# One decode step of attention beside a gated feed-forward: a scheduled kernel, and the same kernel programmed by hand with its own semaphores

## The chip, the cores and the metric

The kernel runs on one core of a Trainium2 chip. The metric is the device time of one execution in microseconds (us). The core has five engines that run their own instruction streams: PE (TensorE, matmuls), DVE (VectorE), ACT (ScalarE), POOL (GpSimd) and SP (SyncE, which here only issues transfers). Sixteen DMA engines move data from DRAM into the on-chip buffer SBUF, whose 128 partitions hold a row of each tile. PSUM is the small memory that matmuls write to.

## The reference, cut to what matters

```
x: (1, 1, 576)   k_cache, v_cache: (1, 32, 16384, 128)
wq: (576, 4096)  wo: (4096, 576)  w_gate, w_up: (576, 4608)  w_down: (4608, 576)     all float32

xn = layernorm(x)
q  = (xn @ wq) per head (32 heads of 128)
p  = softmax(q . k_cache * 128**-0.5)            # over 16384 positions, per head
o  = p @ v_cache
attention   = concat(o) @ wo
feedforward = (gelu(xn @ w_gate) * (xn @ w_up)) @ w_down
out = x + attention + feedforward
```

K and V are 8.39 MB each per head and are read once; with the weights (50.7 MB) that makes 587.6 MB.

## The kernel before

The kernel is written in a tile framework: pools give the buffers, and a scheduler puts in the semaphores. SBUF holds three big buffers of 64 KB a partition: `kslot` twice and `vslot` once. The pools put them at bytes 27904, 93440 and 158976 of a partition, each 256 bytes past a multiple of 512. All big loads are issued by SP, in the order of the program, through `load` (L78); a load whose buffer is still in use holds up those behind it.

First come the weights for q, gate and up. xn is spread over the partitions, PE computes q and the two halves of the feed-forward (`project`, L148), and ACT keeps q in `qrow`.

Then the loop over the 32 heads. K of head h goes into a K buffer, with 128 positions in each partition, in one load (the first head's in two halves of `SUB` = 64 positions). V of head h-1 is loaded into the V buffer right behind it; V of the last head goes into a K buffer instead. The steps of a head:

- `qk`: DVE multiplies K in place by q (L224), which `q_spread` (L163, PE) and `q_take` (L168, ACT) have spread over all partitions for four heads at a time, and sums over the 128 columns into the scores s (L225).
- `softmax`: DVE takes the maximum of s (L229), PE transposes it (L231), DVE takes the maximum over partitions, negated (L233), PE spreads that (L235), ACT scales it (L237) and computes the exponentials into pe (L238).
- `pv`: 32 matmuls on PE (L245) sum p times V into a PSUM bank po. Four heads share a bank: pe is laid out in steps of 16 columns, so that each head's results come to other partitions. There are two banks in turn.
- `out_heads`, after every fourth head: ACT copies the bank (L250), and four small matmuls pick the heads' outputs (L254), which ACT copies into `oall` (L255).

The tail loads w_down (36 rows of 576 a partition) and wo, and adds up rows times hT or oT on PE (L290). Two of the 32 rows of wo in each partition are loaded in another layout, the extra rows: fourteen small loads to 3, 6 or 8 partitions (`load_extra` L309, L320), which DVE sums up (L359, L362). The last rows of wo come in ever smaller loads. x is added at the end, and ACT issues the output.

Of the kernel before, what the change touches and what calls it, by code (L numbers as in the profile page):

```python
# [17 lines left out]
SUB = 64  # L18
# [4 lines left out]
HALF = D // 2  # L23
HD = H * DH
# [6 lines left out]
WD_PIECES = (16, 20)  # L31
WO_PIECES = (8, 8, 6, 4, 2, 1, 1)
WO_A = 8
WO_Q = 8
WO_M = 30
EX_K = 6
EX_H = 4 * EX_K
EX_REST = tuple((s, EX_H + 3 * i) for s in range(2) for i in range(2))
EX_LAST = H - 2
EX_N = 12  # L40
QUART = D // 4
HG = 4
PW = 4 * HG
PAD = 40
QH = 4
# [3 lines left out]
def kernel(ctx: ExitStack, tc: tile.TileContext, x, k_cache, v_cache, wq, wo, wg, wu, wd, out):  # L49
    nc = tc.nc  # L50
    cpool = ctx.enter_context(tc.tile_pool(name="cpool", bufs=1))
    kpool = ctx.enter_context(tc.tile_pool(name="kpool", bufs=2))
    vpool = ctx.enter_context(tc.tile_pool(name="vpool", bufs=1))
    spool = ctx.enter_context(tc.tile_pool(name="spool", bufs=2))
    ps_acc = ctx.enter_context(tc.tile_pool(name="ps_acc", bufs=1, space=bass.MemoryType.PSUM))
    ps_big = ctx.enter_context(tc.tile_pool(name="ps_big", bufs=1, space=bass.MemoryType.PSUM))
    ps_o = ctx.enter_context(tc.tile_pool(name="ps_o", bufs=1, space=bass.MemoryType.PSUM))
    ps_s = ctx.enter_context(tc.tile_pool(name="ps_s", bufs=2, space=bass.MemoryType.PSUM))
# [8 lines left out]
    wox = wo.rearrange("(h r t) f -> t h r f", r=4, t=WO_T)[WO_M:]  # L67
    wol = wo.rearrange("(p t) f -> t p f", t=WO_T)[WO_M:]
# [8 lines left out]
    def load(dst, src):  # L77
        nc.sync.dma_start(dst, src)  # L78
        return dst

    ROW3 = 3 * DF
    wq_t, wg_t, mix = kslot(), kslot(), vslot()
    load(wq_t, wmain["q"])
    qt = load(wg_t[:, ROW3 : ROW3 + QS], wtail["q"])
    row3, tails, at = {}, {}, 0
    for n in "gu":
        row3[n] = load(mix[:, at : at + DF], wmain[n][:, ROW3:])
        tails[n] = load(mix[:, at + DF : at + DF + DF // 2], wtail[n])
        at += DF + DF // 2

    xrow = mix[:1, ROW3 + FG : ROW3 + FG + D]
    nc.scalar.dma_start(xrow, xf)
    x2 = cpool.tile([P, HALF], F32, name="x2")
    nc.gpsimd.memset(x2, 0.0)
    for i in range(2):
        nc.scalar.dma_start(x2[32 * i : 32 * i + 1, :], xf[:, i * HALF : (i + 1) * HALF])

    ident = cpool.tile([P, P], F32, name="ident")
    make_identity(nc, ident)
    ones = cpool.tile([P, P], F32, name="ones")  # L100
    nc.vector.memset(ones, 1.0)
    eps_t = cpool.tile([P, 1], F32, name="eps_t")
    nc.vector.memset(eps_t, EPS)
    par = cpool.tile([P, 2], F32, name="par")
    nc.vector.tensor_reduce(par, ident.rearrange("p (d s) -> p s d", s=2), axis=AX.X, op=ALU.add)
    same = cpool.tile([P, 32], F32, name="same")
    nc.vector.tensor_reduce(same, ident.rearrange("p (q r) -> p r q", q=4), axis=AX.X, op=ALU.add)
    quarter = cpool.tile([P, 4], F32, name="quarter")
    nc.vector.tensor_reduce(quarter, ident.rearrange("p (q r) -> p q r", q=4), axis=AX.X, op=ALU.add)

    st = cpool.tile([1, 2, nc.vector.BN_STATS_DIM], F32, name="st")
    for i in range(2):
        nc.vector.bn_stats(st[:, i, :], xrow[:, i * HALF : (i + 1) * HALF])
    mv = cpool.tile([1, nc.vector.BN_AGGR_DIM], F32, name="mv")
    nc.vector.bn_aggr(mv, st)
    std = cpool.tile([1, 1], F32, name="std")
    nc.scalar.activation(std, mv[:, 1:2], AF.Sqrt, bias=eps_t[:1], scale=1.0)
    rstd = cpool.tile([1, 1], F32, name="rstd")
    nc.vector.reciprocal(rstd, std)
    nc.vector.tensor_scalar(xrow, xrow, mv[:, 0:1], rstd, op0=ALU.subtract, op1=ALU.mult)  # L120
    px = ps_s.tile([P, 512], F32, tag="sm", name="px")
    xm = xrow[:, :DM].rearrange("o (p j) -> o j p", j=DJ)
    for j in range(DJ):
        nc.tensor.matmul(px[:, j : j + 1], xm[:, j, :], ones[:1, :1], start=True, stop=True)
    xd = mix[:1, ROW3 + 2 * FG : ROW3 + 2 * FG + 2 * (D - DM)].rearrange("o (d s) -> o d s", s=2)
    nc.vector.tensor_copy(xd, xrow[:, DM:].unsqueeze(2).to_broadcast([1, D - DM, 2]))
    nc.tensor.matmul(px[:, DJ : DJ + 1], xd.rearrange("o d s -> o (d s)"), ones[:1, :1], start=True, stop=True)
    xp = cpool.tile([P, DJ + 1], F32, name="xp")
    nc.vector.tensor_copy(xp, px[:, : DJ + 1])
    xnb = cpool.tile([P, DJ, 32], F32, name="xnb")  # L130
    nc.vector.tensor_copy(xnb, xp[:, :DJ].unsqueeze(2).to_broadcast([P, DJ, 32]))
    xt = cpool.tile([P, 2], F32, name="xt")
    nc.vector.tensor_scalar(xt, par, xp[:, DJ:], None, op0=ALU.mult)
    xtb = cpool.tile([P, 2, 32], F32, name="xtb")
    nc.vector.tensor_copy(xtb, xt.unsqueeze(2).to_broadcast([P, 2, 32]))

    def project(steps, group, sizes):
        pg = ps_big.tile([P, 3, 512], F32, tag="pb", name="pg")
        for k, (j, rhs) in enumerate(steps):
            for b, size in enumerate(sizes):  # L140
                for q in range(4):
                    lo = q * group + sum(sizes[:b])
                    if j < DJ:
                        lhs = xnb[:, j, :]
                    else:
                        lhs = xtb[:, q // 2, :]
                        lo -= q // 2 * 2 * group
                    nc.tensor.matmul(pg[32 * q : 32 * q + 32, b, :size], lhs, rhs[:, lo : lo + size],  # L148
                                     start=k == 0, stop=k == len(steps) - 1)
        return pg  # L150

    steps = [(DJ, qt)] + [(j, wq_t[:, j * HD : (j + 1) * HD]) for j in range(DJ)]
    pq = project(steps, QG, (QB, QB))[:, :2, :]
    qrow = cpool.tile([P, QG], F32, name="qrow")
    nc.scalar.activation(qrow.rearrange("p (b f) -> p b f", f=QB), pq, AF.Copy)

    Q = {}

    def q_spread(h):
        r = 32 * (h // (H // 4))  # L160
        lo = h % (H // 4) * DH
        pq = ps_s.tile([P, 512], F32, tag="sm", name="pq")
        nc.tensor.matmul(pq, ones[r : r + 1, :], qrow[r : r + 1, lo : lo + QH * DH], start=True, stop=True)  # L163
        return pq

    def q_take(h, pq):
        qs = spool.tile([P, QH, DH], F32, name="qs", bufs=1)
        nc.scalar.activation(qs.rearrange("p h d -> p (h d)"), pq, AF.Copy)  # L168
        for i in range(QH):
            Q[h + i] = qs[:, i : i + 1, :]  # L170
# [87 lines left out]
    for h in range(H + 1):  # L258
# [12 lines left out]
        if h == 0:  # L271
            ffn_act()
# [139 lines left out]
```

## Time and profile before

| | |
|---|---|
| time, median of 3 runs | 1366.81 us (1366.80 to 1368.43) |
| span of the profiled execution (no other time is listed for it) | 1366.7 us |
| DVE busy | 1146.5 us, 84% |
| PE busy | 402.5 us, 29% |
| ACT busy | 36.8 us, 3% |
| load queue q1 | 587.60 MB, 99.4% of 16 engines' span |
| mean rate of reading | 430 GB/s |

The page lists busy times, DMA queues and groups of instructions; the timeline lists single instructions with their start and duration, and in brackets how long the engine had been idle before and what released it. A row of "SPq" or "ACTq" is the issue of a transfer, and the transfer's landing shows as the start of the instruction that waited for it. "x64" for 32 matmuls is right: a float32 matmul is two passes.

### The profile page before, as it was taken

To read this page: it belongs to the slowest core of one execution; us is meant where nothing else is said; L and a number is where in the kernel's file an instruction comes from. 1 tells how busy PE (TensorE), PEld (TensorE's weight loads), DVE (VectorE), ACT (ScalarE), POOL (GpSimd) and SP (SyncE) were. 2 spreads that over 40 slices of the span, in tenths; PEclk is the share of its full clock that TensorE was granted. 3 is DMA by queue.
4 is the path that set the end of the run, shared out by engine and by line. 5 is a ranking of instruction groups with operands and counts; after the bars stand their busy time and mean duration, and the time that the engine had idled before them with its cause. 6 is when DMAs were issued, how large, how long until landed. Compare 5 with 4: busy or idle time off the path is not lost.

```text
span 1366.7 us, 6440 instructions
## 1 busy us (share of the span) xinstructions
PE 402.5 (29%) x2876; PEld 119.1 (9%) x2876; DVE 1146.5 (84%) x189; ACT 36.8 (3%) x129; POOL 1.6 (0%) x8
## 2 busy tenths in 40 slices
PE   3331132332322232332212332322212232322164
PEld 1110000100000000100000000100000000000021
DVE  1069999989888888899888888898888888998843
ACT  0000000000000000000000000000000000000000
POOL 0000000000000000000000000000000000000000
PEclk9775655655655566555555566566556656566578
DMA  9999999999999999999999999999999999999997
GB/s 406 439 441 437 428 430 430 436 430 442 435 428 432 441 432 432 436 435 432 430 440 430 436 432 442 432 430 433 428 437 436 443 430 430 428 435 436 443 421 316
DMA packets 12180, 588.00 MB, mean 430 GB/s; under 512 B 1395, under 2 KB 1401, under 8 KB 2042
## 3 DMA queue, kind: packets, MB, share of 16 engines
q1 hardware_dynamic: 12140, 587.60, 99.4%
q8 instruction: 22, 0.36, 0.1%
q14 instruction: 4, 0.03, 0.0%
q10 hardware_dynamic: 14, 0.01, 0.0%
HBM read 587.60 MB, written 0.00 MB: 430 GB/s over the span
## 4 chain that ended last, share of the span: by engine, by line
DMA 52%; DVE 46%; PE 1%; issue 0%; SPq 0%; DVEq 0%; ACT 0%
DMA kslot<-in_A_k_cache_dram 41%; DVE s L225 23%; DVE kslot L224 23%; DMA kslot<-in_A_v_cache_dram 3%; DMA kslot<-in_B_w_up_dram 3%; DMA kslot<-in_B_w_down_dram 2%; DMA kslot<-in_A_wq_dram 2%; DMA kslot<-in_A_wo_dram 1%; PE pg L148 1%; SPq L78 0%; PE pt L231 0%; DVE vslot L185 0%; SPq L309 0%; DVE pm L229 0%; DVE nm L233 0%
## 5 line engine op out<-in xcount | busy, mean ns | idle before, releaser
L224 DVE TENSOR_TENSOR kslot<-kslot,qs 128x16384 f32<-128x16384 f32 (+1 forms) x33 | 551.3, 16705 | 83.6 <-DMA kslot<-in_A_k_cache_dram 83.6
L225 DVE TENSOR_REDUCE s<-kslot 128x128 f32<-128x16384 f32 (+1 forms) x33 | 551.2, 16703 | 3.7 <-DVE kslot L224 0.5
L245 PE MATMUL po<-vslot,pe 128*16 128x512 f32 x1984 | 285.5, 740 | 632.6 <-DMA vslot<-in_A_v_cache_dram 632.6
L245 PEld LDWEIGHTS po<-vslot,pe 128*16 128x16 f32 x1984 | 67.3, 113 | 835.3 <-issue 835.3
L231 PE MATMUL pt<-ident,pm 128*1 128x128 f32 x32 | 11.9, 372 | 244.5 <-DVE pm L229 244.5
L185 DVE TENSOR_TENSOR vslot<-pg,same 128x396 f32<-128x396 f32 (+1 forms) x6 | 3.0, 551 | 70.2 <-PE pg L148 70.2
L148 PE MATMUL pg<-kslot,xnb 128*32 128x396 f32 (+2 forms) x208 | 22.0, 583 | 21.1 <-DMA kslot<-in_B_w_gate_dram 17.8
L237 ACT ACTIVATE nb<-pb 128x1 f32<-128x1 f32 x32 | 5.5, 171 | 808.4 <-PE pb L235 808.4
L231 PEld LDWEIGHTS pt<-ident,pm 128*1 128x1 f32 x32 | 2.5, 79 | 267.9 <-DVE pm L229 227.0
L235 PE MATMUL pb<-nm,ones 1*128 1x1 f32 x64 | 18.1, 350 | 13.2 <-DVE nm L233 13.2
L233 DVE TENSOR_REDUCE nm<-pt 1x1 f32<-1x128 f32 x32 | 8.9, 279 | 15.0 <-PE pt L231 15.0
L235 PEld LDWEIGHTS pb<-nm,ones 1*128 1x128 f32 x64 | 15.8, 305 | 22.2 <-DVE nm L233 11.3
L163 PE MATMUL pq<-qrow,ones 1*128 1x512 f32 x16 | 15.6, 1073 | 0.0
L359 DVE TENSOR_SCALAR qrow<-qrow,ex 32x576 f32<-32x576 f32 x1 | 0.5, 507 | 15.4 <-DMA qrow<-in_A_wo_dram 15.4
L238 ACT ACTIVATE pe<-s,nb 128x128 f32<-128x128 f32 x32 | 12.8, 402 | 1.0
L329 DVE RECIPROCAL rl<-pl 128x32 f32<-128x32 f32 x1 | 0.4, 358 | 13.7 <-PE pl L327 13.7
L250 ACT ACTIVATE o<-po 128x512 f32<-128x512 f32 x8 | 4.8, 597 | 220.8 <-PE po L245 220.8
L148 PEld LDWEIGHTS pg<-kslot,xnb 128*32 128x32 f32 x208 | 7.1, 124 | 36.5 <-DMA kslot<-in_B_w_gate_dram 18.6
L254 PE MATMUL pc<-same,o 128*128 128x4 f32 x64 | 8.4, 255 | 5.7 <-ACT o L250 5.7
L229 DVE TENSOR_REDUCE pm<-s 128x1 f32<-128x128 f32 x32 | 9.2, 286 | 1.1
L362 DVE SCALAR_TENSOR_TENSOR qrow<-vslot,ex,qrow 24x576 f32<-24x576 f32 (+1 forms) x12 | 9.7, 806 | 0.4
L290 PE MATMUL acc<-kslot,oT 128*1 128x144 f32 (+1 forms) x108 | 8.5, 334 | 3.1 <-DMA kslot<-in_A_wo_dram 3.1
(89 smaller groups left out, 123.1 us busy)
## 6 DMA issues: line engine op xcount, KB each, us to landing
kslot<-in_A_k_cache_dram SPq DMA_DIRECT2D x2, 4096.0 KB
kslot<-in_B_w_gate_dram SPq DMA_DIRECT2D x1, 6912.0 KB
kslot<-in_B_w_up_dram SPq DMA_DIRECT2D x1, 6912.0 KB
kslot<-in_B_w_down_dram SPq DMA_DIRECT2D x1, 5760.0 KB
vslot<-in_B_w_down_dram SPq DMA_DIRECT2D x1, 4608.0 KB
kslot<-in_A_wo_dram SPq DMA_DIRECT2D x2, 2304.0 KB
vslot<-in_B_w_gate_dram SPq DMA_DIRECT2D x1, 2304.0 KB
vslot<-in_B_w_up_dram SPq DMA_DIRECT2D x1, 2304.0 KB
```

Of the source, the lines that this page charges most:

```text
L148: nc.tensor.matmul(pg[32 * q : 32 * q + 32, b, :size], lhs, rhs[:, lo : lo + size], start=k == 0, stop=k == len(steps) - 1)
L163: nc.tensor.matmul(pq, ones[r : r + 1, :], qrow[r : r + 1, lo : lo + QH * DH], start=True, stop=True)
L224: tc.keep_in_program_order(nc.vector.tensor_mul(blk, blk, Q[h].to_broadcast([P, n, DH])))
L225: nc.vector.tensor_reduce(S[h][:, i : i + n], blk, axis=AX.X, op=ALU.add)
L229: tc.keep_in_program_order(nc.vector.reduce_max(pm, S[h], axis=AX.X))
L231: nc.tensor.transpose(pt[:1, :P], pm, ident)
L233: tc.keep_in_program_order(nc.vector.tensor_reduce(nm, pt[:1, :P], axis=AX.X, op=ALU.max, negate=True))
L235: nc.tensor.matmul(pb[:, :1], ones[:1, :], nm, start=True, stop=True)
L238: nc.scalar.activation(pe4, S.pop(h).rearrange("p (k s) -> p k s", s=4), AF.Exp, bias=nb, scale=SCALE, accum_out=lsum[:, h : h + 1])
L245: nc.tensor.matmul(PO[h // HG % 2][q : q + PW, :], pe[:, lo : lo + PW], vt[:, k * 512 : (k + 1) * 512], start=i == 0 and k < 4, stop=i == ...
L290: tc.keep_in_program_order(nc.tensor.matmul(g, lhs, w[:, i * n : (i + 1) * n], start=id(g) not in seen, stop=last))
L362: nc.vector.scalar_tensor_tensor(ex_sum[:n], ex_rows[j][:n], ex[:n, j : j + 1], ex_sum[:n], op0=ALU.mult, op1=ALU.add)
```

## The change

The framework's scheduler is left aside. Every buffer has a fixed address, the three big ones (`A`, `B`, `C`) at 28672, 94208 and 159744, multiples of 4096 bytes. Each engine's program is written out by itself, with semaphores of its own: `take` waits for a semaphore and counts it down, `give` counts it up, and `done` makes an engine wait for its own last instruction. SP, ACT, PE and DVE loop over the heads (`Fori`; SP and DVE two heads to a trip), with the head's number in a register. K goes to B (even heads) and A (odd heads), V to C, the last V too. The first K is one load. q is spread a head at a time: ACT picks one head's q from all of them (`q_pick`), PE spreads it (`q_spread`), ACT copies it to qs. pe has no gaps and PO is one bank; each head's output is copied and picked by itself. There are no extra rows of wo: all 32 rows go through PE, w_down into B and A, wo into A and C.

SP's list of transfers at the end of the loop over the heads and in the tail. Before, where K30, V29, K31, V30 and V31 come first:

```order
L78 DMA kslot<-in_A_k_cache_dram 128x16384 [waits DMAHW5_49,DVE_49]
L78 DMA vslot<-in_A_v_cache_dram 128x16384 [waits DMAHW0_49,PE_49]
L78 DMA kslot<-in_A_v_cache_dram 128x16384 [waits DMAHW7_49,DVE_49]
L309 DMA vslot<-in_A_wo_dram 6x4x576 [waits DMAHW2_49,PE_49]
L309 DMA vslot<-in_A_wo_dram 6x4x576 x3
L78 DMA vslot<-in_B_w_down_dram 128x9216
```

(The first of these rows is K31, the third V31, and the small loads of wo and the first part of w_down follow.) After, from the end of SP's loop, where fa, fb and fv say that slot A, B or C is free:

```order
L129 DMA slot_a<-in_A_k_cache_dram 128x16384
L129 DMA slot_c<-in_A_v_cache_dram 128x16384 [waits fv_13]
L213 REGISTER_ALU
L213 COMPARE_AND_BRANCH
L129 DMA slot_c<-in_A_v_cache_dram 128x16384 [waits fv_13]
L129 DMA slot_b<-in_B_w_down_dram 128x16128 [waits fb_12]
L129 DMA slot_a<-in_B_w_down_dram 128x4608 [waits fa_11]
L129 DMA slot_a<-in_A_wo_dram 128x11520
L129 DMA slot_c<-in_A_wo_dram 128x3456 [waits fv_13]
```

V31 (the first row behind the loop) waits for the buffer that V30 is in, no longer for a K buffer, and w_down stands behind it.

DVE's work for a head in the body, before:

```order
L224 TENSOR_TENSOR kslot<-kslot,qs 128x16384 [waits DMAHW7_49]
L225 TENSOR_REDUCE s<-kslot 128x128 [waits DVE_49,Activation_49]
L229 TENSOR_REDUCE pm<-s 128x1 [waits DVE_49]
L233 TENSOR_REDUCE nm<-pt 1x1 [waits PE_49]
L224 TENSOR_TENSOR kslot<-kslot,qs 128x16384 [waits DMAHW1_49]
```

After, one trip of its loop (kb and ka: K has landed, qr: q is spread, sf: given by PE's first V matmul of the head before):

```order
L188 TENSOR_TENSOR slot_b<-slot_b,qs 128x16384 [waits kb_9,qr_33]
L191 TENSOR_REDUCE s<-slot_b 128x128 [waits own_63,sf_39]
L193 TENSOR_REDUCE pm<-s 128x1 [waits own_63]
L195 TENSOR_REDUCE nm<-bank 1x1 [waits pt_35]
L188 TENSOR_TENSOR slot_a<-slot_a,qs 128x16384 [waits ka_8,qr_33]
L191 TENSOR_REDUCE s<-slot_a 128x128 [waits own_63,sf_39]
L193 TENSOR_REDUCE pm<-s 128x1 [waits own_63]
L195 TENSOR_REDUCE nm<-bank 1x1 [waits pt_35]
L331 REGISTER_ALU
L331 COMPARE_AND_BRANCH
```

The reduce waited for ACT's exponentials of the head before, and now waits for PE, whose first V matmul comes behind them and behind V's landing.

The diff, cut to its core:

```diff
-    def kslot():
-        return kpool.tile([P, R * DH], F32, tag="k", name="kslot")
-    def vslot():
-        return vpool.tile([P, R * DH], F32, tag="v", name="vslot")
...
+SLOTS = (28672, 94208, 159744)
+WD_A, WO_A = 28, 20
+WO_C = (6, 3, 2, 1)
+WO_Q = 6
...
+def take(eng, s, n=1):
+    eng.wait_ge(s, n).then_inc(s, -n)
+def give(eng, s, n=1):
+    eng.sem_inc(s, n)
+def done(eng, inst):
+    ...
+    inst.then_inc(s, 1)
+    take(eng, s)
...
+def q_pick(h):
+    ACT.activation(qh, qd4.rearrange("p j t -> p (j t)"), AF.Copy, scale=whose[:, bass.ds(h, 1)]).then_inc(s_r, 1)
+def q_spread():
+    take(PE, s_r)
+    PE.matmul(pqb[:, :DH], ones, qh, start=True, stop=True).then_inc(qp, 1)
+def dve_head(k, slot, s_k, s_f):
+    kt = slot.rearrange("p (n d) -> p n d", d=DH)
+    take(DVE, s_k, 16)
+    take(DVE, qr)
+    done(DVE, DVE.tensor_mul(kt, kt, qs.unsqueeze(1).to_broadcast([P, R, DH])))
+    give(DVE, qd)
+    take(DVE, sf)
+    done(DVE, DVE.tensor_reduce(S, kt, axis=AX.X, op=ALU.add))
+    give(DVE, s_f)
+    DVE.reduce_max(pm, S, axis=AX.X).then_inc(s_pm, 1)
+    take(DVE, s_pt)
+    DVE.tensor_reduce(nm, ptb[:1, :P], axis=AX.X, op=ALU.max, negate=True).then_inc(s_nm, 1)
...
+        take(SP, fB)
+        load(B, kv[0], kB)
+        take(SP, fA)
+        load(A, kv[1], kA)
+        take(SP, fV)
+        load(C, vv[0], vL)
+        with SP.Fori(0, H // 2 - 1) as i:
+            take(SP, fB)
+            load(B, kv[bass.ds(2 * i + 2, 1)].rearrange("a p f -> (a p) f"), kB)
+            take(SP, fV)
+            load(C, vv[bass.ds(2 * i + 1, 1)].rearrange("a p f -> (a p) f"), vL)
+            take(SP, fA)
+            load(A, kv[bass.ds(2 * i + 3, 1)].rearrange("a p f -> (a p) f"), kA)
+            take(SP, fV)
+            load(C, vv[bass.ds(2 * i + 2, 1)].rearrange("a p f -> (a p) f"), vL)
+        take(SP, fV)
+        load(C, vv[H - 1], vL)
+        take(SP, fB)
+        load(B[:, : WD_A * D], wdv[:, : WD_A * D], s_tail[0])
+        take(SP, fA)
+        load(A[:, : (WD_T - WD_A) * D], wdv[:, WD_A * D :], s_tail[1])
+        load(A[:, wo_a : wo_a + WO_A * D], wov[:, : WO_A * D], s_tail[2])
+        take(SP, fV)
+        lo = WO_A
+        for k, n in enumerate(WO_C):
+            load(C[:, (lo - WO_A) * D : (lo - WO_A + n) * D], wov[:, lo * D : (lo + n) * D], s_tail[3 + k])
+            lo += n
...
+        with ACT.Fori(0, H) as h:
+            q_pick(h + 1)
+            take(ACT, qp)
+            take(ACT, qd)
+            ACT.activation(qs, pqb[:, :DH], AF.Copy).then_inc(qr, 1)
+            take(ACT, s_pb)
+            done(ACT, ACT.activation(nb, ptb[:, 256:257], AF.Copy, scale=SCALE))
+            ACT.activation(pe, S, AF.Exp, bias=nb, scale=SCALE, accum_out=lsum[:, bass.ds(h, 1)]).then_inc(s_ex, 1)
+            take(ACT, s_pv)
+            ACT.activation(o4, PO, AF.Copy).then_inc(s_o4, 1)
+            take(ACT, s_pc)
+            done(ACT, ACT.activation(oall[:, bass.ds(h, 1)], pcb[:, :1], AF.Copy))
...
+        with DVE.Fori(0, H // 2):
+            dve_head(0, B, kB, fB)
+            dve_head(1, A, kA, fA)
...
+        with PE.Fori(0, H):
+            q_spread()
+            take(PE, s_pm)
+            PE.transpose(ptb[:1, :P], pm, ident).then_inc(s_pt, 1)
+            take(PE, s_nm)
+            PE.matmul(ptb[:, 256:257], ones[:1, :], nm, start=True, stop=True).then_inc(s_pb, 1)
+            take(PE, s_ex)
+            take(PE, vL, 16)
+            for k in range(32):
+                q = 32 * (k % 4)
+                i = PE.matmul(PO[q : q + 4, :], pe[:, 4 * k : 4 * k + 4], C[:, k * 512 : (k + 1) * 512],
+                              start=k < 4, stop=k >= 28)
+                if k == 0:
+                    i.then_inc(sf, 1)
+            i.then_inc(s_pv, 1)
+            take(PE, s_o4)
+            for j in range(4):
+                i = PE.matmul(pcb[:, :1], o4[:, j * DH : (j + 1) * DH], same[:, j : j + 1], start=j == 0, stop=j == 3)
+                if j == 0:
+                    i.then_inc(fV, 1)
+            i.then_inc(s_pc, 1)
```

More of the change, by code (lines that the diff above doesn't have):

```diff
@@ L58, with small @@
-    ps_s = ctx.enter_context(tc.tile_pool(name="ps_s", bufs=2, space=bass.MemoryType.PSUM))
+    PE, DVE, ACT, SP, PL = nc.tensor, nc.vector, nc.scalar, nc.sync, nc.gpsimd
+    at = {"low": LOW, "high": HIGH}
+    def small(name, shape, where="low"):
+        n = 4
+        for s in shape[1:]:
+            n *= s
+        h = nc.alloc_sbuf_tensor_at(name, list(shape), F32, offset=at[where])
+        at[where] += (n + 31) // 32 * 32
+        assert at["low"] <= SLOTS[0] and at["high"] <= 229344
+        return h.ap()
@@ new lines, in slot @@
+    def slot(name, i):
+        return nc.alloc_sbuf_tensor_at(name, [P, SLOT], F32, offset=SLOTS[i]).ap()
+    A, B, C = slot("slot_a", 0), slot("slot_b", 1), slot("slot_c", 2)
+    bank = [nc.alloc_psum_tensor(f"bank{i}", [P, 512], F32).ap() for i in range(8)]
+    ident = small("ident", [P, P])
+    ones = small("ones", [P, P])
+    x2 = small("x2", [P, HALF])
+    eps_t = small("eps_t", [P, 1])
+    par = small("par", [P, 2])
+    same = small("same", [P, 32])
+    quarter = small("quarter", [P, 4])
@@ L157 @@
[L157 to L170, printed above, removed]
```

515 lines of the change are left out of this document (237 added, 278 removed).

## Prediction

> **What bounds the kernel now.** First the parts of the page on engines and DMA queues.
>
> ```profile
> span 1366.7 us, 6440 instructions
> ...
> PE 402.5 (29%) x2876; PEld 119.1 (9%) x2876; DVE 1146.5 (84%) x189; ACT 36.8 (3%) x129; POOL 1.6 (0%) x8
> ...
> q1 hardware_dynamic: 12140, 587.60, 99.4%
> q8 instruction: 22, 0.36, 0.1%
> ```
>
> Queue q1, where SP puts all its loads, keeps the 16 DMA engines busy for 99.4% of the span (1358 us); DVE, the busiest compute engine, has 16% left. The table of windows says how fast the stream is in the body (first row) and in the last two stages; the last two numbers of a row are DMA share and GB/s.
>
> ```profile
> 307.30:1237.50 930.20, 258.59 (x1668) 71.62 (x1668) 840.23 (x97) 24.18 (x90) 0.00 (x0) 0.61 1.00 434
> ...
> 1295.50:1314.80 19.30, 10.63 (x67) 2.83 (x67) 15.72 (x3) 0.67 (x3) 0.00 (x0) 0.68 0.98 423
> 1314.80:1363.10 48.30, 31.54 (x386) 12.42 (x386) 12.53 (x25) 1.24 (x6) 0.00 (x0) 0.83 0.91 383
> ```
>
> In the body the queue never rests: share 1.00 at 434 GB/s. The last window has 0.91: there some engines rest. Then the list of waits, and the row of the V matmuls:
>
> ```profile
> DVE kslot L224 <- DMA kslot<-in_A_k_cache_dram: 83.6, 27, 4.4
> PE po L245 <- DMA vslot<-in_A_v_cache_dram: 632.6, 31, 23.1
> ...
> L245 PE MATMUL po<-vslot,pe 128*16 128x512 f32 x1984 | 285.5, 740 | 632.6 <-DMA vslot<-in_A_v_cache_dram 632.6
> ```
>
> DVE and PE wait for K and V, not the reverse. So the time is bytes over rate plus every moment in which the queue has nothing to do, and the change has to be judged by one question: when does it let the queue run dry? One head from the timeline shows the margins.
>
> ```profile
> 496.44 0.33 SPq L78 DMA_DIRECT2D kslot<-in_A_k_cache_dram  x1
> ...
> 500.55 17.23 DVE L224 TENSOR_TENSOR kslot<-kslot,qs 128x16384 f32<-128x16384 f32 x1 [3.08 <-DMA kslot<-in_A_k_cache_dram]
> 517.88 17.22 DVE L225 TENSOR_REDUCE s<-kslot 128x128 f32<-128x16384 f32 x1
> ...
> 519.96 8.34 PE L245 MATMUL po<-vslot,pe 128*16 128x512 f32 x64 [20.35 <-DMA vslot<-in_A_v_cache_dram]
> ...
> 528.36 0.33 SPq L78 DMA_DIRECT2D vslot<-in_A_v_cache_dram  x1
> 535.13 0.33 SPq L78 DMA_DIRECT2D kslot<-in_A_k_cache_dram  x1
> 535.14 0.29 DVE L229 TENSOR_REDUCE pm<-s 128x1 f32<-128x128 f32 x1
> ...
> 535.89 0.28 DVE L233 TENSOR_REDUCE nm<-pt 1x1 f32<-1x128 f32 x1 [0.47 <-PE pt L231]
> ...
> 539.21 17.22 DVE L224 TENSOR_TENSOR kslot<-kslot,qs 128x16384 f32<-128x16384 f32 x1 [3.05 <-DMA kslot<-in_A_k_cache_dram]
> ...
> 558.55 9.52 PE L245 MATMUL po<-vslot,pe 128*16 128x512 f32 x64 [21.69 <-DMA vslot<-in_A_v_cache_dram]
> ```
>
> A K lands at 500.55, a V at 519.96, the next K at 539.21, the next V at 558.55: 19.3 us each, 38.6 a head (16.78 MB at 434 GB/s). The V issued at 528.36 comes 10.8 us before the transfer ahead of it is done (539.21); the K issued at 535.13 comes 23.4 before 558.55.
>
> **The body after the change.** Two waits move.
>
> The V buffer now comes free only after ACT has copied PO and PE has done the first of four picking matmuls, every head. The tail of before shows both at L250 and L254 (rows below): 0.72 us from the last V matmul to the picks, and a quarter of 1.05 us. So V is issued 1.0 us later, with 9.8 of 10.8 left: nothing, as long as K's transfer covers it; past that each us would cost 31, one for every V.
>
> The reduce of head h now waits for the first V matmul of head h-1 (semaphore sf). Behind it on DVE stand the maximum, the negation and the next product; SP's next K waits for it too. At 740 ns a pass, two passes overlapping, I take 1.0 us: the reduce starts at 521.0 instead of 517.88, ends at 538.2, and maximum, transpose and negation (535.14 to 536.17 in before) end at 539.3. The next K is there at 539.21, so the next product starts 0.1 to 0.5 late, ends by 557, and the reduce behind it waits for V anyway (558.55 + 1.0). The lag does not grow. K is issued near 538.3, 20 us early. DVE's own work for a head is 34.45 + 1.03 + gaps, about 35.8; the engine's waits on itself (the gap at 517.78 to 517.88 is 0.1) may make that 36.2. That leaves 2.4 us a head, 4.9 per trip of DVE's loop, which takes two heads.
>
> Spreading q each head puts a pick and a copy on ACT and a small matmul on PE behind the V matmuls. Bounded by the rows of the 512-wide spread and copy of before
>
> ```profile
> L163 PE MATMUL pq<-qrow,ones 1*128 1x512 f32 x16 | 15.6, 1073 | 0.0
> ...
> 518.22 0.60 ACT L168 ACTIVATE qs<-pq 128x512 f32<-128x512 f32 x1 [19.37 <-DVE kslot L224]
> ```
>
> this is at most 0.6 + 1.1 + 0.6 after 528.3 + 0.7 + 1.05 + 0.2, so qs is ready by 532.6, 6.6 us before the product at 539.21. Nothing either, and below nothing is excluded, since the queue is already full.
>
> **The start.** K0 is one load, not two halves, so DVE starts on the whole.
>
> ```profile
> 0.74 0.85 SPq L78 DMA_DIRECT2D kslot<-in_A_wq_dram  x2
> ...
> 75.55 7.63 PE L148 MATMUL pg<-kslot,xnb 128*32 128x396 f32 x72 [3.38 <-DMA kslot<-in_B_w_up_dram]
> ...
> 121.80 0.33 SPq L78 DMA_DIRECT2D kslot<-in_A_k_cache_dram  x1
> ...
> 133.56 8.69 PE L245 MATMUL po<-vslot,pe 128*16 128x512 f32 x64 [8.79 <-DMA vslot<-in_A_v_cache_dram]
> ```
>
> The up weights land at 75.55, K0 19.3 later at 94.9; product and reduce end near 129.7, and K2 is issued there instead of at 121.80. V0 lands at 133.56, 3.9 us later. An issue into an empty queue needs a lead. The chain of waits prices it:
>
> ```profile
> 1.18 23.69 DMA kslot<-in_A_wq_dram
> 24.86 0.14 issue
> ```
>
> Issued from 0.74, the 9.44 MB of wq are there at 24.86: 24.1 us, where 434 GB/s would need 21.7, so 2.4 us of lead. 3.9 covers it: cost 0, at most 1. From there DVE is a buffer behind and gains 2.4 a head; K3 (issued near 165.6, V1 due at 172.2) is already safe. The entry of the hand-written part has one more meeting of the engines: 0 to 0.7 us. Fewer instructions to fetch: all 0.36 MB of q8 are 0.8 us of the stream, so 0 to -0.8. I take nought for these together.
>
> **The tail** is where the change bites.
>
> ```profile
> 1272.06 0.33 SPq L78 DMA_DIRECT2D kslot<-in_A_v_cache_dram  x1
> ...
> 1295.51 9.68 PE L245 MATMUL po<-vslot,pe 128*16 128x512 f32 x64 [21.78 <-DMA vslot<-in_A_v_cache_dram]
> ...
> 1305.25 3.27 SPq L309 DMA_DIRECT2D vslot<-in_A_wo_dram  x4
> ...
> 1314.84 8.55 PE L245 MATMUL po<-kslot,pe 128*16 128x512 f32 x64 [2.49 <-DMA kslot<-in_A_v_cache_dram]
> ...
> 1323.46 0.60 ACT L250 ACTIVATE o<-po 128x512 f32<-128x512 f32 x1 [10.37 <-PE po L245]
> 1324.11 1.05 PE L254 MATMUL pc<-same,o 128*128 128x4 f32 x8 [0.72 <-ACT o L250]
> ...
> 1357.25 0.41 PE L290 MATMUL acc<-kslot,oT 128*1 128x288 f32 x2 [1.36 <-DMA kslot<-in_A_wo_dram]
> ...
> 1357.49 0.41 PE L290 MATMUL acc<-kslot,oT 128*1 128x288 f32 x2
> ...
> 1363.13 0.43 PE L290 MATMUL acc<-kslot,oT 128*1 128x144 f32 x8 [0.28 <-DMA kslot<-in_A_wo_dram]
> ```
>
> Before, the last V (V31) goes into a K buffer: issued at 1272.06, it follows V30 without a gap (1295.51, 1314.84). After, it goes into slot C, where V30 is being used, and SP's queue is in order: the weights of the tail, whose slot B has long been free, stand behind V31's wait. Between V30's landing and V31's issue nothing is queued. V31 is issued after PE's matmuls of head 30 and the copy and pick: 1295.51 + 9.68 + 1.0 = 1306.2. It starts an empty queue, so it lands 2.4 + 19.3 later, at 1327.9 instead of 1314.84: **+13.1**. Ends: the matmuls took 8.34 to 9.68 in the rows shown, and the lead may be down to 1.0, since part of the 2.4 may belong to the very first transfer. That gives 10.4 to 13.1, and I take the upper, whose rows are nearest.
>
> What follows V31 are wd and wo, 20.05 MB. Before takes 1314.84 to 1363.13, 48.3 us, in the window of share 0.91, among them fourteen loads into 3 to 8 partitions each. After has loads of 128 partitions only, all but the last four queued behind V31 before it lands, those four when V31 is used up, some 38 us ahead of their turn: 46.2 us at 434 GB/s, **-2.1**. Ends: nought, and -4.3 if the whole idle 9% of the window comes back. PE does not become late: two rows of weights take 0.24 us (1357.25 to 1357.49), so the 20 rows of wo that now land together need 2.4, at half pace 4.8, while the 12 rows behind them stream for 8.2. From the last landing to the end it is as before, 1366.7 - 1363.13 = 3.6.
>
> **Sum:** 1366.7 + 13.1 - 2.1 = **1377.7** (1327.9 + 46.2 + 3.6). The span is 0.1 below the median of the runs, so the same holds for the time.
>
> **Rivals.** *The aligned buffers pay for the gap.* Before has all three slots 256 bytes past a multiple of 512; after has them at multiples of 4096. If this alone made the stream 1% faster, 1358 us would shrink by 13.6 and the time would be 1364.1, faster than before. It decides from 0.8% (11.0 of 1358). For it: no transfer of before is aligned, so no row excludes it. Against it: the body stands at one steady rate with share 1.00. [...] Chance 0.02 for faster, 0.04 for a gain that lands within 0.2%.
>
> *The loops become the bound.* If each trip of DVE's loop (two heads) had to fetch its instructions again, one block of q8 costs 0.1% of 16 x 1366.7 over 22 blocks, 1.0 us, and 2.4 of lead, 3.4 in all: under the 4.9 that DVE has to spare. Two blocks in turn are 6.8, 1.9 too long, times 16 trips: 30 us, about 1408. [...] Chance 0.08.
>
> *The gap is covered all the same*, because the tail regains the 4.3, the lead is 1.0 and the matmuls 8.3: 1366.7 + 10.4 - 4.3 = 1372.8, still slower; only with a gain in the stream beside it would this be no change. Chance 0.02 for that.
>
> **The numbers.** Forecast 0.84, slow loops 0.08, the rest 0.08. About 0.2% (2.7 us) is what a measurement can tell from no change: faster 0.03, same 0.05, slower 0.92. The range takes in the low ends of the tail (1372.8) and, above, a tail that regains nothing with the start's 1.0 and 0.7 (1381.5), widened by the spread of a run or so: 1372 to 1383. The loops lie outside.
>
> **What would show it.** Right: in the windows a body at share 1.00 and 434, then a hole of about 12 us between the landing of V30 and the first bytes of V31, with SP waiting for PE; DVE's reduce waiting on PE for 3 us a head. Wrong: share below 0.99 in the body (loops, or a buffer freed late), a rate above 437 (alignment), or V31 landing 19.3 us after V30.

## The result, and the profile after

The hand-written kernel is slower by 1.2%.

| | before | after |
|---|---|---|
| time, median | 1367.62 us (1366.80 to 1368.44, 4 runs) | 1383.91 us (1382.73 to 1384.42, 4 runs) |
| ratio, with 95% interval | | 1.0116 (1.0101 to 1.0130) |
| span of the profiled execution | 1366.7 us | 1381.9 us (time 1383.64) |

First the page of after: engines, the moved gigabytes in 40 slices, and the queues.

```profile
span 1381.9 us, 8013 instructions
...
PE 442.0 (32%) x3104; PEld 171.5 (12%) x3104; DVE 1141.0 (83%) x173; ACT 71.5 (5%) x231; POOL 1.0 (0%) x7
...
GB/s 401 435 442 419 435 429 438 425 438 431 436 434 433 438 431 434 438 427 438 434 433 438 431 436 433 433 440 429 436 438 427 438 431 436 436 431 438 258 413 320
...
q1 hardware_dynamic: 11376, 587.60, 98.4%
q8 instruction: 5, 0.08, 0.0%
```

DVE stays as it was (83% of the span); PE and ACT do a little more and have most of the span free (32% and 5% busy). The queue does not stay: 99.4% of the span has become 98.4%, and one slice near the end stands at 258 GB/s. The table of windows is cut at that place. The moments of the first and last bytes, here and below, are from the trace's single DMA records, which no view prints; the last three numbers of a row are granted PE clock, DMA share and GB/s.

```profile
307.30:1237.50 930.20, 283.60 (x1849) 111.45 (x1849) 844.84 (x98) 50.73 (x168) 0.00 (x0) 0.61 1.00 434
...
1293.90:1306.60 12.70, 11.00 (x72) 4.25 (x72) 10.24 (x1) 0.77 (x2) 0.00 (x0) 0.76 0.00 0
...
1358.30:1367.00 8.70, 0.02 (x3) 0.05 (x7) 0.00 (x0) 0.00 (x0) 0.00 (x0) 0.68 0.91 392
1367.00:1374.20 7.20, 7.20 (x84) 2.38 (x88) 0.00 (x0) 0.00 (x0) 0.00 (x0) 0.67 0.86 356
```

From 307 us on, the body has the share and the rate of before (1.00, 434). Then comes a window of 12.7 us without a byte. In the last two rows PE is idle for 8.7 us and then busy for all of 7.2, at 0.67 of its clock. The timeline of after names both places. ("<-PEq L118" only says that the engine's own program waited in `take`, which is L118; for which semaphore stands in the program. "x48" merges rows of two forms: six rows in halves, four matmuls each, and three in quarters, eight each.)

```profile
1294.34 9.98 PE L377 MATMUL bank<-slot_c,pe 128*4 128x512 f32 x64 [17.18 <-PEq L118]
...
1304.45 0.60 ACT L266 ACTIVATE o<-bank 128x512 f32<-128x512 f32 x1 [26.30 <-ACTq L118]
1305.19 1.02 PE L384 MATMUL bank<-same,o 128*128 128x1 f32 x8 [0.87 <-PEq L118]
1305.65 0.34 SPq L129 DMA_DIRECT2D slot_c<-in_A_v_cache_dram  x1
1306.10 0.36 SPq L129 DMA_DIRECT2D slot_b<-in_B_w_down_dram  x1
...
1327.63 8.60 PE L377 MATMUL bank<-slot_c,pe 128*4 128x512 f32 x64 [11.87 <-PEq L118]
...
1366.98 7.37 PE L401 MATMUL bank<-slot_a,oT 128*1 128x288 f32 x80 [8.69 <-PEq L118]
1374.17 2.36 PE L401 MATMUL bank<-slot_c,oT 128*1 128x288 f32 x48
...
1377.54 0.92 PE L401 MATMUL bank<-slot_c,oT 128*1 128x144 f32 x24
1378.63 0.31 DVE L347 COPY ot<-bank 128x144 f32<-128x144 f32 x1 [1.59 <-DVEq L118]
```

V30 lands at 1294.34; V31 is issued at 1305.65, when PE is through with V30 and the first pick (L384) has given the slot back; w_down (slot_b), whose buffer was free all along, follows at 1306.10. V31 lands at 1327.63. At the end the 20 rows of wo keep PE from 1366.98 to 1374.17, so that at 1374.87, when the last byte comes, it has only begun the nine rows before the last three.

### The profile page after: what moved, and what is told of

Read it like the earlier page. It is cut to its first block, busy times and chain, and to the rows that moved or that the text cites. A ratio compares the mean times of both kernels' runs of the same rounds, so it can differ in the third digit from the quotient of the medians.

```text
span 1381.9 us, 8013 instructions
## 1 busy us (share of the span) xinstructions
PE 442.0 (32%) x3104; PEld 171.5 (12%) x3104; DVE 1141.0 (83%) x173; ACT 71.5 (5%) x231; POOL 1.0 (0%) x7
## 3 DMA queue, kind: packets, MB, share of 16 engines
q1 hardware_dynamic: 11376, 587.60, 98.4%
## 5 line engine op out<-in xcount | busy, mean ns | idle before, releaser
L377 PE MATMUL bank<-slot_c,pe 128*4 128x512 f32 x2048 | 296.4, 738 | 491.6 <-PEq L118 491.6
L191 DVE TENSOR_REDUCE s<-slot_a 128x128 f32<-128x16384 f32 x16 | 275.5, 17220 | 35.5 <-DVEq L118 35.5
L191 DVE TENSOR_REDUCE s<-slot_b 128x128 f32<-128x16384 f32 x16 | 275.5, 17220 | 31.5 <-DVEq L118 31.5
L188 DVE TENSOR_TENSOR slot_b<-slot_b,qs 128x16384 f32<-128x16384 f32 x16 | 275.6, 17225 | 8.4 <-DVEq L118 8.4
L188 DVE TENSOR_TENSOR slot_a<-slot_a,qs 128x16384 f32<-128x16384 f32 x16 | 275.6, 17226 | 0.0
L377 PEld LDWEIGHTS bank<-slot_c,pe 128*4 128x4 f32 x2048 | 84.7, 99 | 676.2 <-issue 664.5
L266 ACT ACTIVATE o<-bank 128x512 f32<-128x512 f32 x32 | 19.1, 597 | 761.1 <-ACTq L118 761.1
L384 PE MATMUL bank<-same,o 128*128 128x1 f32 x256 | 32.7, 249 | 28.3 <-PEq L118 28.3
L384 PEld LDWEIGHTS bank<-same,o 128*128 128x128 f32 x256 | 31.0, 191 | 57.1 <-issue 57.1
L182 PE MATMUL bank<-qh,ones 128*128 128x128 f32 x66 | 20.4, 402 | 54.6 <-PEq L118 54.6
```

Of the source, the lines that this page charges most:

```text
L182: PE.matmul(pqb[:, :DH], ones, qh, start=True, stop=True).then_inc(qp, 1)
L188: done(DVE, DVE.tensor_mul(kt, kt, qs.unsqueeze(1).to_broadcast([P, R, DH])))
L191: done(DVE, DVE.tensor_reduce(S, kt, axis=AX.X, op=ALU.add))
L266: ACT.activation(o4, PO, AF.Copy).then_inc(s_o4, 1)
L377: i = PE.matmul(PO[q : q + 4, :], pe[:, 4 * k : 4 * k + 4], C[:, k * 512 : (k + 1) * 512], start=k < 4, stop=k >= 28)
L384: i = PE.matmul(pcb[:, :1], o4[:, j * DH : (j + 1) * DH], same[:, j : j + 1], start=j == 0, stop=j == 3)
```

## The experiments

All in one table; the span is the median of a kernel's runs, "last byte" and "end behind it" are of its profile. The first four runs of after have a median span of 1382.15, the second four, which the differences below start from, 1380.9: a difference of 1 us between two sets of four is not clear of the noise. Before was run beside each: its spans have a median of 1366.4 us (19 runs in the first set), in two groups near 1365 and 1366.4.

| kernel | time | ratio to before (95%) | span | last byte | end behind it |
|---|---|---|---|---|---|
| before | 1368.15 | | 1366.4 | 1362.75 | 4.0 |
| after, run again | 1382.77 | 1.0107 (1.009 to 1.0123) | 1380.9 | 1374.71 | 6.9 |
| V31 in slot B | 1369.21 | 1.0011 (1.0001 to 1.002) | 1367.45 | 1360.12 | 7.4 |
| w_down ahead of V31 | 1369.84 | 1.002 (1.001 to 1.0031) | 1367.7 | 1360.25 | 6.0 |
| wo in pieces | 1381.46 | 1.0101 (1.0084 to 1.0118) | 1379.7 | 1374.19 | 5.4 |
| V31 in B, wo in pieces | 1366.81 | 0.9993 (0.9984 to 1.0002) | 1365.0 | 1359.79 | 5.5 |
| the same, filled (4 groups) | 1366.68 | 0.9990 (0.9981 to 0.9999) | 1364.9 | 1360.76 | 4.7 |
| the same, filled (1 group) | 1382.72 | 1.0109 (1.0093 to 1.0124) | 1380.95 | 1359.67 | 20.5 |
| before, V31 in its V buffer | 1371.64 | 1.0033 (1.0021 to 1.0045) | 1369.85 | 1365.95 | 4.0 |
| the same, order forced | 1382.0 | 1.0102 (1.0086 to 1.0118) | 1380.2 | 1375.80 | 4.1 |
| loops written out | 1386.79 | 1.0138 (1.0122 to 1.0153) | 1384.9 | 1377.62 | 6.8 |
| slots unaligned | 1382.7 | 1.0114 (1.0097 to 1.0131) | 1380.95 | 1374.26 | 6.9 |
| reduce released by ACT | 1382.72 | 1.0106 (1.009 to 1.0122) | 1380.65 | 1373.69 | 6.8 |

**V31 into slot B.** w_down's first part goes to C instead, and the last rows of wo to B.

```diff
-        take(SP, fV)
-        load(C, vv[H - 1], vL)
         take(SP, fB)
-        load(B[:, : WD_A * D], wdv[:, : WD_A * D], s_tail[0])
+        load(B, vv[H - 1], vZ)
+        take(SP, fV)
+        load(C[:, : WD_A * D], wdv[:, : WD_A * D], s_tail[0])
...
-        with PE.Fori(0, H):
+        with PE.Fori(0, H - 1):
+            pe_head(C, vL)
+        pe_head(B, vZ)
```

> The last V goes into slot B, free since head 30's reduce, and w_down's first part into C. My theory (the hole in the queue behind V30 costs 13 to 14 us, and PE is late in the tail besides): V31 lands 19.3 us after V30, near 1313.7 instead of 1327.6, and everything behind it comes as much earlier: span near 1368.0. Rival (the cost lies in the body, its loops, semaphores or per-head work): V31's place changes little, span near 1381.

The windows of this run, from V30's landing to V31's, and to the last byte:

```profile
1294.40:1313.70 19.30, 11.22 (x74) 4.16 (x74) 16.80 (x1) 1.45 (x4) 0.00 (x0) 0.68 1.00 434
1313.70:1360.10 46.40, 29.76 (x311) 10.20 (x315) 3.29 (x9) 1.63 (x6) 0.00 (x0) 0.75 0.96 411
```

V31 comes 19.3 us behind V30 at share 1.00, and the last byte comes 14.75 us earlier than in after. The span is 1367.5 in the profile: the rival with its 1381 falls. But the last byte is now 2.6 us earlier than in before, and the span is 1.0 longer: the end behind the last byte, 7.4 against 4.0, is a second cost.

**w_down ahead of V31.** V31 stays in slot C; only the order of two issues is changed.

```diff
-        take(SP, fV)
-        load(C, vv[H - 1], vL)
         take(SP, fB)
         load(B[:, : WD_A * D], wdv[:, : WD_A * D], s_tail[0])
+        take(SP, fV)
+        load(C, vv[H - 1], vL)
```

> V31 stays in slot C, but w_down's first part (8.26 MB, 19.0 us) is put ahead of it in SP's queue. My theory: it is what fills the hole, so that the share of the queue stays at 1.00 up to V31; V31 lands near 1294.3 + 19.0 + 19.3 = 1332.6 and the last bytes near 1360; PE then has w_down, wo and head 31 all behind V31 and ends some us later than its last transfer, span 1364 to 1369. Rival (V31 late is itself the cost, since head 31's chain follows it): span 1382 or more, since V31 lands 5 us later than in the kernel after.

The timeline of PE in this run:

```profile
1332.48 8.84 PE L377 MATMUL bank<-slot_c,pe 128*4 128x512 f32 x64 [16.89 <-PEq L118]
...
1344.57 6.97 PE L401 MATMUL bank<-slot_b,hT 128*1 128x288 f32 x112 [0.22 <-PEq L118]
...
1353.75 5.03 PE L401 MATMUL bank<-slot_a,oT 128*1 128x288 f32 x80
1358.60 2.37 PE L401 MATMUL bank<-slot_c,oT 128*1 128x288 f32 x48
```

V31 lands at 1332.5, five us later than in after, and the span is 13 us shorter. So V31's lateness costs nothing by itself; the empty queue does. PE has hardly a pause from 1344.57 on (granted clock 1.00), and the 20 rows that took 7.37 us in after take 5.03. The runs spread more than others (spans of 1365.9 to 1370.6), which stays unexplained.

**Before, with V31 in its V buffer.** The same wait, put into the scheduled kernel.

```diff
-            VT[h - 1] = load(vslot() if h < H else kslot(), vv[h - 1])
+            VT[h - 1] = load(vslot(), vv[h - 1])
...
-    ta, tb, te = vslot(), kslot(), kslot()
+    ta, tb, te = kslot(), kslot(), vslot()
```

> The kernel before with one edit: its last V goes into the V buffer, and w_down's first part with the extra rows into the K buffer that V31 had. My theory (this wait alone costs the hole, in either kernel): no bytes between V30's landing and about 1306, V31 lands 12 to 13 us later than at 1314.8, span 1378 to 1380. Rival (the hand-written program has further costs of several us that the early landing of V30 or the loads without extra rows hide): here the hole costs less than 10 us, span under 1376.

The median span is 3.5 us longer than before's (one of the six runs had 1375.0): the number is the rival's, the reason is not. SP's queue in the timeline shows it:

```profile
1272.57 0.33 SPq L78 DMA_DIRECT2D kslot<-in_B_w_down_dram  x1
1305.73 0.33 SPq L78 DMA_DIRECT2D vslot<-in_A_v_cache_dram  x1
```

The scheduler saw that V31 had to wait and put w_down's first part ahead of it, at 1272.57. Its bytes lasted until 1306.43, and the queue stood empty for 0.26 us. The next run forces the order:

```diff
+                tc.keep_in_program_order(nc.sync.dma_start(VT[h - 1], vv[h - 1]))
...
-    wd_rows = load_rows(ta, 0, wdv, 0, a)
+    tc.keep_in_program_order(nc.sync.dma_start(ta[:, : a * D], wdv[:, : a * D]))
+    wd_rows = [ta[:, j * D : (j + 1) * D] for j in range(a)]
```

> The kernel before again with its last V in the V buffer, and now with the order of the loads written out: w_down's first part behind V31, as the hand-written kernel has it (in the run without this the scheduler had put w_down ahead of V31: the queue stood idle for 0.26 us only, and the last byte came at 1365.95). My theory (the hole is the order of SP's queue, whoever wrote the kernel): idle from about 1295.5 to 1306.7, V31 lands near 1328, last byte 12.5 to 13.5 us behind the 1362.75 of before, span 1379 to 1380.5. Rival (the hand-written program has other costs that add to it): a hole as long, but a span under 1377.

SP's queue in the timeline of this run:

```profile
1304.81 0.33 SPq L268 DMA_DIRECT2D vslot<-in_A_v_cache_dram  x1
1305.23 3.26 SPq L313 DMA_DIRECT2D kslot<-in_A_wo_dram  x4
1308.53 0.44 SPq L317 DMA_DIRECT2D kslot<-in_B_w_down_dram  x1
```

Now the queue is empty from 1295.11 to 1305.78, V31 lands at 1326.8, and the span is 1380.2: 13.9 us over before (1366.3 beside it). In the hand-written kernel the same wait is worth 13.5 (1380.9 against 1367.45). It belongs to the order of the loads, not to the way the rest is written.

**wo in pieces.** In the kernel after, the 20 rows in slot A come as three loads.

```diff
+WO_P = (8, 6, 6)
...
-        load(A[:, wo_a : wo_a + WO_A * D], wov[:, : WO_A * D], s_tail[2])
+        for k, n in enumerate(WO_P):
+            load(A[:, wo_a + lo * D : wo_a + (lo + n) * D], wov[:, lo * D : (lo + n) * D], s_wo[k])
+            lo += n
```

> The 20 rows of wo in slot A come as three loads (8, 6 and 6 rows) with a semaphore each instead of one. My theory (PE is late in the tail because 20 rows are released at once, 7.37 us of work of which the first part runs at half clock): the first rows start near 1359, PE is through the 20 rows by about 1368, and the end follows the last landing by 3.5 us: span 1378.5 to 1379.5, 2.4 to 3.4 less than the 1381.9 of the kernel after. Rival (the last landing at 1375 sets the end): no change, 1381.5 to 1382.3.

PE's timeline of this run, with three of the five groups of rows of wo:

```profile
1358.23 2.12 PE L407 MATMUL bank<-slot_a,oT 128*1 128x288 f32 x32 [0.88 <-PEq L119]
...
1366.41 3.06 PE L407 MATMUL bank<-slot_a,oT 128*1 128x288 f32 x24 [2.25 <-PEq L119]
...
1370.51 4.00 PE L407 MATMUL bank<-slot_c,oT 128*1 128x288 f32 x48 [1.04 <-PEq L119]
```

The median span is 1.2 us below the second four runs of after (2.4 below the first four), 2.3 in the profiles; I expected 2.4 to 3.4. By itself this is not clear of the noise, since the four runs here spread over 3.0 us (1377.9 to 1380.9); the same edit with V31 in B, below, is 10 runs against 11. The rows start when they land, but PE, idle in between, is at half clock again (granted 0.50 from 1363.7 to 1373.8): six rows take 3.06 us at 1366.41, and the last nine 4.00, where the run with w_down ahead has 2.37.

**Both edits.** 

> V31 into slot B (as in the run with only that edit, whose last byte came at 1360.1) and the 20 rows of wo in three loads (which brought the end from 7.0 to 5.4 us behind the last byte). My theory (the two costs are separate and add up): last byte near 1360.1, end 5 to 5.5 us later, span 1365.1 to 1365.6; the kernel before has 1366.7 in its profile. Rival (with V31 early, PE stands idle longer before wo and runs at half clock whatever the pieces): no better than V31 alone, 1367.5.

As expected: 1365.3 in the profile, 1365.0 as the median span, 2.4 below V31 in B alone and 1.4 below before. By times the interval (0.9984 to 1.0002) holds no change as well.

**Filling PE's pauses** in the kernel with both edits.

```diff
+FILL = {8: 14, 14: 14, 20: 14, 26: 6, 29: 3}
...
+            for _ in range(FILL.get(j, 0)):
+                PE.matmul(bank[4][:1, :HALF], ident[:, :1], C[:, :HALF], start=True, stop=True)
```

> The kernel with both edits, and while PE waits for the pieces of wo it does 51 one-row matmuls whose result nobody uses (0.12 us each at full clock; 14, 14, 14, 6 and 3 of them before the second to sixth piece). My theory (the end is late because PE, a third busy, runs at half clock when the last rows land): granted clock 1.0 in the last 15 us instead of about 0.65, the last nine-row group takes 2.4 us instead of 4.0, end 4 us behind the last byte as in the kernel before, span near 1364.2. Rival (the clock does not matter, or the filling itself delays the rows): the same as without the filling or longer, 1365.3 or more.

The first filling (L429) in the timeline:

```profile
1345.59 6.71 PE L429 MATMUL bank<-slot_c,ident 128*1 128x288 f32 x27
```

A miss of mine in the size: 27 passes took 6.71 us, 0.25 each, and PE became the bound, 20.5 us behind the last byte. The real rows go to four groups of 32 columns in turn; the filling had one. Spread as they are (`bank[4][q : q + 1]` with q = 0, 32, 64, 96 in turn):

> The filling again, spread over four groups of 32 columns of TensorE as the real rows are (in the run with one group each pass took 0.25 us, 28 of them 6.9 us, and the rows were late). At 0.06 us a pass the 14 fillings take 1.7 us, less than the 2.6 us that a six-row piece leaves. My theory: granted clock 1.0 in the last 15 us, end 4 us behind the last byte, span near 1364.0. Rival: no gain over the kernel without filling, whose median span is 1365.0, or a loss.

The first filling (L430) in the timeline of this run, and its last two windows:

```profile
1346.91 2.11 PE L430 MATMUL bank<-slot_c,ident 128*1 128x288 f32 x28
```

```profile
1355.00:1360.00 5.00, 4.46 (x80) 1.93 (x74) 0.90 (x2) 0.00 (x0) 0.00 (x0) 1.00 0.70 288
1360.00:1365.00 5.00, 2.10 (x50) 0.90 (x40) 0.31 (x1) 0.00 (x0) 0.00 (x0) 1.00 0.03 7
```

The same 28 passes take 2.11 us, and the clock is 1.00 to the end (0.73 and 0.50 in these two windows without filling). But the span is what it was, 1364.9 against 1365.0: the end comes 4.7 instead of 5.5 us behind the last byte, and in the profile the last byte came 1.0 us later. 0.3 of that was there when V31 landed, before the first filling (1313.62 against 1313.32 in the DMA records); whether the filling caused the rest was not tried. So with the rows in pieces the half clock costs at most about 1 us, less than I thought.

**Loops written out**: every `Fori` replaced by a loop that leaves constants.

```diff
-        with DVE.Fori(0, H // 2):
+        for _ in range(H // 2):
...
-        with PE.Fori(0, H):
+        for _ in range(H):
```

> The kernel after with the loops over the heads of SP, ACT, DVE and PE written out, every index a constant. My theory (the loops cost nothing, and save the queue the fetching of instructions that brought V30 1.2 us earlier): instruction queue back near 0.36 MB, V30 lands 0 to 1.2 us later, span 1381.9 to 1383.1. Rival (the loops' branches cost time that the wait for K hides in the body but that shows at its ends): span 1381 or less, and the pauses between DVE's steps shorter.

The queues on the page of this run, and V30's landing in its timeline:

```profile
q1 hardware_dynamic: 11376, 587.60, 98.2%
q8 instruction: 25, 0.41, 0.1%
```

```profile
1298.07 9.03 PE L377 MATMUL bank<-slot_c,pe 128*4 128x512 f32 x64 [17.16 <-PEq L118]
```

The direction was right, the size not: V30 lands 3.7 us later than in after, and the median span is 4.0 longer (1384.9 against 1380.9). Twenty more fetches of instructions than after has (25 packets, 0.41 MB) cost five times their bytes at 434 GB/s (0.33 MB, 0.8 us). V's landings fall behind after's in steps: by 0.9 us at 406, 2.1 at 522, 3.5 at 1101, 3.7 at V30. The DMA records show how. Each big transfer ends with sixteen records of 4 bytes, which I take as one from each DMA engine. In the body they come again every 19.32 us; with each fetch between 370 and 1270 us their sixteen times shift by 1.43 us in sum (after the fetch at 449.3, one record moves by 1.1 us). At V30 the first of the sixteen is 0.3 us later than in after, the last 3.7 (1292.19 and 1297.65 against 1291.88 and 1293.92). So in this run a fetch held back about one engine, and the load landed with the slowest.

**Slots unaligned, and the reduce released by ACT.** The first takes the addresses of before; the second gives `sf` after the exponentials.

```diff
-SLOTS = (28672, 94208, 159744)
+SLOTS = (27904, 93440, 158976)
```

> The kernel after with its three slots at 27904, 93440 and 158976, where the kernel before has them. My theory (alignment is worth nothing, the body streams 434 GB/s in both): span 1381.5 to 1382.3. Rival (alignment to 4096 gains something that the hole in the tail hides): span longer by over 3 us, 1385 or more, with less than 434 GB/s in the body.

```diff
-            ACT.activation(pe, S, AF.Exp, bias=nb, scale=SCALE, accum_out=lsum[:, bass.ds(h, 1)]).then_inc(s_ex, 1)
+            done(ACT, ACT.activation(pe, S, AF.Exp, bias=nb, scale=SCALE, accum_out=lsum[:, bass.ds(h, 1)]))
+            give(ACT, s_ex)
+            give(ACT, sf)
...
-                if k == 0:
-                    i.then_inc(sf, 1)
```

> The kernel after, with ACT's exponentials instead of PE's first V matmul releasing the reduce of the next head, as in the kernel before. My theory (that wait lies beside the stream and costs nothing): the reduce starts within 0.2 us of the product's end instead of 2.7 behind it, DVE then waits for K instead, span the same, 1381 to 1382.5. Rival (the wait shortens the lead with which K is issued and so costs something in the body): span 1380 or less.

Spans of 1380.95 and 1380.65 stood 1.2 to 1.5 under the four runs of after, so after was run again:

> The kernel after once more, unchanged, as the measure for the two runs that changed one thing in its body or its addresses (median spans 1380.95 with the slots where the kernel before has them, and 1380.65 with the reduce released by ACT; four runs of after had 1381.0 to 1382.5). If those two edits are worth nothing, as my theory has it, this run's median span is 1380.5 to 1381.3; if each gained over a us, as a rival would have it, it is 1382 or more again.

Its median is 1380.9: neither edit shows a gain or a loss. The window of the unaligned body has the same share and rate as after's, and in the timeline of the other run (second fence) the reduce starts 0.35 us behind the product while the next product waits for K:

```profile
307.30:1237.50 930.20, 281.17 (x1849) 116.71 (x1849) 844.61 (x98) 50.70 (x168) 0.00 (x0) 0.62 1.00 434
```

```profile
519.91 17.22 DVE L191 TENSOR_REDUCE s<-slot_a 128x128 f32<-128x16384 f32 x1 [0.35 <-DVEq L118]
...
540.98 17.23 DVE L188 TENSOR_TENSOR slot_b<-slot_b,qs 128x16384 f32<-128x16384 f32 x1 [2.37 <-DVEq L118]
```

## Why the prediction was right or wrong

The direction and the main cause held; the time, 1383.91 against 1377.7, lies 0.9 above the range. Two steps make the miss: PE at the end (+3.4 us) and the span taken as the time (+1.7). By the prediction's own terms:

| step | predicted | measured | difference |
|---|---|---|---|
| V31 lands | 1327.9 | 1327.63 | -0.3 |
| from there to the last byte | 46.2 | 47.2 | +1.0 |
| from the last byte to the end of the span | 3.6 | 7.0 | +3.4 |
| from the span to the time | 0 | 1.7 | +1.7 |
| the profiled execution to the median | 0 | 0.3 | +0.3 |

(The forecast's last landing is PE's start at 1363.13 in before, 0.4 us behind the last byte there; that much belongs in the second row and not in the third.)

**The body: right.** Share 1.00 and 434 GB/s, K and V 19.3 us apart. The list of waits of after (us in total, times, longest) has the new wait, which by the program is for PE's first V matmul; 3 us a head were forecast, 2.1 came on average:

```profile
DVE s L191 <- DVEq L118: 67.0, 32, 2.7
```

Releasing the reduce earlier changed nothing (1380.65 against 1380.9), so those 67 us lie beside the stream.

**The start and the fetches: both taken too small, in opposite directions.** K2 is issued at 130.45 and V0 lands at 133.72, as forecast, but the queue does not keep its pace: from 113 to 330 us it moves 430 GB/s where before moves 434, and V5 lands 1.8 us later than in before (V1 1.1). First before, then after:

```profile
113.00:330.00 217.00, 58.45 (x364) 16.56 (x368) 207.40 (x31) 5.60 (x22) 0.57 (x1) 0.59 1.00 434
```

```profile
326.70 9.40 PE L245 MATMUL po<-vslot,pe 128*16 128x512 f32 x64 [21.77 <-DMA vslot<-in_A_v_cache_dram]
```

```profile
113.00:330.00 217.00, 62.50 (x396) 24.04 (x400) 209.02 (x24) 11.24 (x39) 0.00 (x0) 0.59 1.00 430
```

```profile
328.46 9.94 PE L377 MATMUL bank<-slot_c,pe 128*4 128x512 f32 x64 [14.43 <-PEq L118]
```

The 3.9 us of lead were counted to V0's landing. By the 4-byte records the first engine is through with V0 at 131.52, 1.1 us after K2's issue, and over K2 the sixteen lose about 1 us on average. That the short lead costs this is a reading, since no run issued K2 earlier, and where the rest is lost is open. Then before, which fetches 14 blocks of instructions from 334 to 1262 us where after fetches none, falls back by 2.9 us, and V30 lands 1.2 earlier in after (1294.34 against 1295.51). "Nought for these together" came out near by luck.

**The wait for slot C: right**, in place, size and cause. 12.7 us of empty queue, then a first transfer of 20.5 us instead of 19.3. From V30's landing to V31's it is 33.3 us, 0.9 more than forecast; V30's 1.2 hide that in the table. Taking the wait away gave 13.5 back; putting it into before cost 13.9.

**"PE does not become late": wrong,** and the larger miss. The step read two rows of weights into the 0.24 us from 1357.25 to 1357.49. The timeline of before, with the rows of po that stand between those of acc:

```profile
1357.25 0.41 PE L290 MATMUL acc<-kslot,oT 128*1 128x288 f32 x2 [1.36 <-DMA kslot<-in_A_wo_dram]
1357.26 0.41 PE L290 MATMUL po<-kslot,oT 128*1 128x288 f32 x2
1357.49 0.41 PE L290 MATMUL acc<-kslot,oT 128*1 128x288 f32 x2
```

Four matmuls start in 0.24 us, and a row of wo is four: two groups of 288 columns, each in two passes. (acc and po hold two rows, but only one pass of each.) So 0.24 us are one row, and "x80" is 20 rows. Twenty rows need 4.8 us at full clock (these rows were granted 1.00; with w_down ahead, without a pause and at 1.00, they took 5.03). At half clock they would need about 8.7, an estimate from the 44 of the 80 passes that start in after in 4.78 us granted 0.50; they took 7.37 after a pause of 8.7 us. The 8.2 us in which the last 12 rows stream were to cover 2.4 to 4.8, and had to cover 7.4 with nine more rows behind. In pieces the end comes 1.5 us nearer to the last byte, 1.9 with V31 in B; filling the pauses as well brings 0.8 more, and the last 0.7 over before stays open.

**The remainder: right.** By the DMA records the 20.05 MB behind V31 took 48.4 us in before, 46.4 and 46.5 in the two runs with V31 in slot B, and 47.7 in after. So between landings the 2.1 us of the forecast are saved; that it is the loads of 128 partitions that save them fits, but no run changed these loads alone. The 1.3 us by which after falls behind the runs with slot B lie in the counting: there the sixteen records that end V31 are spread over 2.4 us (1311.29 to 1313.74), so that most engines are ahead with w_down when it lands, and behind the empty queue they lie within 0.5 (1326.64 to 1327.14). From the mean of the sixteen the rest takes 47.9 us with V31 in B and 48.0 in after.

**The span as the time: wrong.** In before, the profile's 1366.7 was taken to be the time less 0.1. Every run of before listed later has a time 1.74 to 1.85 us above its span. The profiled execution was one of the longer group (span near 1366.4, time near 1368.3), and its neighbourhood to the median was chance. With the 1.7 us added the forecast is 1379.4, and a range moved with it holds the result; the 3.4 us of PE are missing all the same.

**The rivals.** Alignment shows no gain (1380.95 against 1380.9). Slow loops fall: five packets on q8, and without loops the kernel is 4.0 us slower. "Fewer instructions to fetch: 0 to -0.8" was too small for the same reason: it is the 2.9 us between V5 and V30.

Of the 14.5 us between the spans (1380.9 against 1366.4), the order of one load is 13.5 by its own run; in the profile of that run what is left is 3.4 for PE at the end, -2.0 for the transfers behind V31, and -0.6 for V31's landing (1313.74 against 1314.35), in which the start and the fetches nearly cancel. Without the first it stands 1.0 over before, and with wo in pieces as well, 1.4 under.

## What to carry to other kernels

Where one queue bounds the time and is issued in order, look at each wait in it for what stands behind: a transfer whose buffer is free should never stand behind one that must wait for a reader. Moving one line, w_down ahead of V31, was worth 13 us although it made V31 itself later. Count what an engine has left to do when the last bytes land in instructions as the trace counts them, and at the clock that it has there; and take the step from span to time from the runs, not from a coincidence.

## What the hardware showed beyond this

- PE worked at half clock after a pause: in after, idle for 8.7 us, it was granted 0.50 for the first 4.8 us of work (1366.98 to 1371.76) and 1.00 from there. Short pieces with gaps had it too (wo in pieces: six rows 3.06 us after a gap of 2.3, granted 0.50, against 1.64 at clock 1.00). Such a gap did not always do it: with both edits two pieces after gaps of 1.8 and 2.5 us still took 1.64. With the pauses filled over four groups the clock was 1.00 from 1340 us to the end. How long a pause or how much work it takes to change the clock was not shown.
- One-row matmuls into one group of 32 columns took 0.25 us a pass (27 in 6.71 us), in four groups in turn 0.075 (28 in 2.11 us), both at clock 1.00.
- V31 (8.39 MB), issued into an empty queue, sent its first byte 0.97 us after its issue and its last byte 20.5 us after the first, where a K or V that follows another lands 19.3 us behind it (in both kernels: after, and before with the order forced).
- Twenty fetches of instructions (loops written out) cost 4.0 us of a full queue, five times what their bytes would: the sixteen end records of a load shifted by 1.43 us in sum with each fetch (after the one at 449.3, 1.1 us in a single record), and a load landed with the slowest.
